# First expert blocks from attention step 20 instead of 22, with a wider spacing

## The chip, the cores and the metric

One Trainium2 chip, one of its cores. The metric is the device time of the whole kernel in microseconds, as the median of several runs. The kernel computes an attention layer with spatially reduced keys and, on its output, a mixture of eight experts, of which each row uses one.

## The reference, cut to what matters

```python
# attention: B=4, N=12288 rows, C=128; kv is pooled 4x4 to 768 keys per batch
kv_pool = kv.reshape(B, H // 4, 4, W // 4, 4, C).mean(axis=(2, 4))
k = v = kv_pool.reshape(B, -1, C) @ w_sr
s = (q @ k.transpose(0, 2, 1)) / sqrt(C)
a = softmax(s)
x = (a @ v).reshape(B * N, C)                     # 49152 rows

# experts: E=8, F=1024; each row goes to the expert of its highest logit
logits = (x / |x|) @ (emb / |emb|).T / tau
e = argmax(logits); gate = softmax(logits)[e]
out[row] = gate * (relu(x[row] @ w1[e]) @ w2[e])
```

Products are made from fp16 pairs (a high part and what is left of it), three terms for each.

## The kernel before, in words

The 49152 rows are worked through in 96 **steps** of 512 rows (`NSTEP`), 24 steps for each of the four batches. A step has four chunks of 128 rows. For each chunk TensorE makes the scores against 768 keys (`s_mm`, L608), VectorE takes the row maximum (`s_max`, L613), a small operation turns it into the bias of the exponential (`s_bias`, L625 where it is on VectorE), ScalarE takes the exponential (`s_exp`, L631), the result is cut into a high and a low fp16 part (`p_hi` L649, `p_lo` L659), both are transposed by DMAs of the SP queue (`p_t`, L664), and TensorE multiplies them with the values (`av`, L679). `x_norm` (L690, L691) and `x_mul` (L699 where it is on ScalarE, L701 where it is on VectorE) divide by the row sums. The query of a step is turned either on TensorE (`q_t`, L341) or, from step `qd` on, by a DMA (`q_turn`).

Four steps make a **group**. For each group a chain of small VectorE operations picks the expert of every row (`g_logits` and what follows; its tiles are called n3z, y and so on, with the group's number), and POOL scatters the 16 sets of 128 rows into a buffer in HBM sorted by expert (L183, `xs_rows`). From the third group on, `select` also picks four **tiles**: each a block of 512 rows of one expert that has been filled so far. A tile needs the scatters of its group plus two, is loaded by the SP queue (`load`, L1274) with its weights by POOL (`load_w`, L1258), and has eight units: first product (`l1`, L1298), ReLU high part on ScalarE (`h_hi`, L1305), low part on VectorE (`h_lo`, L1310), second product (`l2`, L1331). Then `o_out` (L1340) scales and POOL scatters the rows to the output (L183, `out_dram`). 88 tiles have 512 rows; after them smaller ones of 256 rows take what is left (18 in this run).

The keys and values of batch 1 are pooled on POOL (L365 to L386) while batch 0 is under way; step 24 needs them.

**The order** of all this is written out by a planner in the kernel's own Python (`Plan.run`): each operation has an engine, an assumed duration and a key, and whenever an engine is free it takes the ready operation of lowest key. The engines then run their lists in that order on the chip. Keys are times in the planner's scale: `TS[k]` is the key of step k, which grows by `da` for each step before `ka` and by `di` after it; `slot(k, s)` is step k plus s eighths; the other entries of `X` are offsets. Up to step `ka` the score tiles have four buffers in PSUM; there `swap_banks` (`x_swap`) gives two of them and one more bank to the experts. `x_swap` waits until the users of those banks are done. Before, tile m has the key of step `ka + m`:

```python
    for m in range(NTILE):
        k = KA + m
        TM.append(TS[k] if k <= NSTEP else TM[-1] + X["db"] * size(m - 1) / T)
```

with `ka=22`, so that 22 steps hold attention alone, 74 steps hold one tile each, and 14 tiles and the small ones follow behind the attention. A letter string in `X` deals an operation to engines: `nm` and `nm0` the bias (mixed steps and steps before `ka`), `xn` and `xn0` the product of `x_mul`, `pm` the two parts of the exponentials in the first steps (A is ScalarE, D VectorE, P POOL).

Of the kernel before, what the change touches and what calls it, by code (L numbers as in the profile page):

```python
# [36 lines left out]


X = dict(
    ka=22, da=6.919, di=15.197, db=12.403, dma=1.46, ahead=3.016, av=9.0, av0=0.39, l2=1.971, qt=5.647,  # L40
    lead=15.443, x=4.072, r=2.598, s=-2.823, p=10.466, x0=18.227, r0=19.685, s0=2.117, p0=10.054, qt0=1.742,
    pm="cabcbcacccbccbccccacaa", pl="aaaaaaaa", nm="DD", xn="A", nm0="D", xn0="DA", we="dcdadcddaddcddcd",
    h=5.625, kv=6.596, kvs=0.535, w0=-23.865, start=21.505, early=28.723, wd=10.527, xw=0.77, qd=45, qs=4.44,
    ql=8.549, v0=47.946, m=1.536, end=-1.246, ne=-9.661, ge=-97.983,
)


# [1 line left out]
def attention_moe(  # L49
# [26 lines left out]
    NSTEP = NT // Q  # L76
# [4 lines left out]
    T, TR = 512, 256  # L81
# [129 lines left out]
    class Plan:  # L211
# [8 lines left out]
        def add(self, eng, dur, key, fn, *deps, dma=None, take=None, free=None, hold=False, lands=False):  # L220
            op = Op(eng, dur, key, fn, deps, dma, take, free, hold, lands, self.stage)
            self.ops.append(op)
            return op
# [94 lines left out]
    pl = Plan()  # L318
# [4 lines left out]
    kvs = pools.enter_context(tc.tile_pool(name="kvs", bufs=1))  # L323
# [930 lines left out]
    def size(t):  # L1254
        return T if t < NA else TR

    def load_w(t):
        nc.gpsimd.indirect_dma_start(  # L1258
            out=wbuf[t % WB][:, :],
            out_offset=None,  # L1260
            in_=wprep[:, :],
            in_offset=bass.IndirectOffsetOnAxis(ap=wi_i[:, t : t + 1].bitcast(U32), axis=0),
            bounds_check=E * P - 1,
            oob_is_err=False,
        )

    def load(t):
        n = size(t)
        o = nc.sync.value_load(off_i[0:1, t : t + 1], min_val=0, max_val=NROW - n)
        x = wk2.tile([P, 2, n], F16, tag="x", name=f"x_{t}", bufs=3)  # L1270
        m = wk2.tile([P, n // P, 2], F32, tag="m", name=f"m{t}", bufs=4)
        src = xs[ds(o, n), :]
        moves = [
            nc.sync.dma_start(out=x[:, h, :], in_=src.bitcast(F16)[:, h * HP : h * HP + C], transpose=True)  # L1274
            for h in range(2)
        ]
        b = nc.sync.dma_start(out=m, in_=src[:, CG : CG + 2].rearrange("(j p) c -> p j c", p=P))
        if t < NA:
            for ins in (*moves, b):
                for key in keys[t // PER + 3 :]:  # L1280
                    tc.declare_no_dep(ins.ins, group=key, reason="rows of earlier groups only")
                tc.add_to_no_dep_group("loads", ins.ins)
        ts[t].update(x=x, m=m)

    def units(t):
        return NF * size(t) // 512

    def l1(t, u):
        n = size(t)
        fu = 512 // n  # L1290
        wt, x = wbuf[t % WB], ts[t]["x"]
        pool = ps_s if t >= NA and u % 2 else ps_h
        ph = pool.tile([P, 512], F32, tag="ph", name=f"ph{t}_{u}")
        for kk in range(fu):
            f = (u * fu + kk) * P
            terms = ((0, x[:, 0, :]), (F, x[:, 0, :]), (0, x[:, 1, :]))
            for i, (o, r) in enumerate(terms):
                nc.tensor.matmul(  # L1298
                    ph[:, kk * n : (kk + 1) * n], wt[:, o + f : o + f + P], r, start=i == 0, stop=i == 2
                )  # L1300
        ts[t]["ph", u] = ph
# [45 lines left out]
    def o_scatter(t, j):  # L1347
        scatter(out, ts[t]["m"][:, j, 1:2].bitcast(U32), ts[t]["o"][:, j, :], NT - 1, "out")


    KA = X["ka"]
    KX = KA - 1
    TS = [0.0]
# [3 lines left out]
    def slot(k, s):  # L1357

        k, s = k + int(s // 8), s % 8
        hurry = X["end"] / X["ne"] * min(max(k + s / 8 - (NSTEP - X["ne"]), 0), X["ne"])  # L1360
        return TS[k] + s / 8 * (TS[k + 1] - TS[k]) - hurry
# [4 lines left out]
    def turn(tag, bufs):  # L1366

        u = uses.setdefault(tag, [])
        return (u[-1][:1] if u else []) + (u[-bufs] if len(u) >= bufs else [])

    def took(tag, op):
        uses[tag].append([op])
        return op

    def reads(tag, *ops):
        uses[tag][-1].extend(ops)
# [6 lines left out]
    early = []  # L1383
# [248 lines left out]
    def group_ops(g, t):  # L1632
        if g == NGRP - 1:
            t -= X["ge"]
        ops = g_logits(g)
        lg = chain(t, 0.3, ops, *counted[g], *placed.get(g - 1, ()), *placed.get(g - 2, ()))
        t += 0.3 * len(ops)
        ex = add("ACT", 0.2, t, lambda: g_exp(g), lg[-1])
        rk = add("PE", 0.02, t, lambda: g_count(g), lg[-1], *chosen.get(g - 5, ()), take=f"rk{g}")
        rk = add("DVE", 0.1, t, lambda: g_counts(g), rk)  # L1640
        rk = add("PE", 0.12, t, lambda: g_rank(g), rk)
        places, gates = g_place(g)
        t += 2.0
        pc = []
        for i, fn in enumerate(places):
            deps = pc[-1:] if i else [rk, *chosen.get(g - 5, ())]
            pc.append(add("DVE", 0.2, t + 0.3 * i, fn, *deps, free=f"rk{g}" if i == 1 else None))
        gc = chain(t + 0.5, 0.3, gates, ex, pc[-1], dur=0.15)
        o = pc[0]
        t += 3.0  # L1650
        sc = [
            add("POOL", 1.28, t + 1.28 * i, lambda i=i: g_scatter(g, i), pc[-1], gc[-1], dma=0.22) for i in range(GT)
        ]
        placed[g] = [pc[-1], gc[-1], *sc]
        b = g * G // SPB
        g_last[b] = [gc[-1]]
        counted["n", g] = o
        if g >= 2:
            n = g - 2
            chosen[n] = []  # L1660
            deps = [o, *(chosen[n - 1][-1:] if n else ())]
            for i, fn in enumerate(select(n, base[(n + 3) % 3])):
                eng, dur = ("DVE", 0.15) if fn.__name__ in SELECT_DVE else ("POOL", 0.3)
                chosen[n].append(add(eng, dur, t + 0.3 * i, fn, *(chosen[n][-1:] or deps)))
        return t

    TM = []
    for m in range(NTILE):
        k = KA + m
        TM.append(TS[k] if k <= NSTEP else TM[-1] + X["db"] * size(m - 1) / T)  # L1670

    def swap_banks(last):
        nonlocal ps_s, ps_h
# [17 lines left out]
    for k in range(NSTEP):  # L1691
        if k % SPB == SPB // 2 and k // SPB + 1 < B:
            kv_ops(k // SPB + 1)
        t = step_ops(k)
        if k % G == G - 1:
            t = group_ops(k // G, t)
    x_last = add("-", 0.0, TS[NSTEP], lambda: swap_banks(True), *uses["s1"][-1], *uses["s1"][-2])
    end = counted["n", NGRP - 1]
# [5 lines left out]
    for t in range(NTILE):  # L1704
        pl.stage = sum(t >= NA + n for n in STAGES)
        s, n, nu = TM[t], t // PER, units(t)
        w = (X["di"] if KA + t < NSTEP else X["db"]) / 8
        whole = t < NA
        deps = [x_open, chosen[n][-1], *placed[n + 2]] if whole else [x_open, rest[-1], x_pads, x_dummies, *placed[NGRP - 1]]
        ld = add("SP", 3.5, s - X["lead"], lambda t=t: load(t), *deps, *turn("mx", 3), *turn("m", 4), dma=1.3 * size(t) / T)  # L1710
        took("mx", ld)
        took("m", ld)
        lw = took("wb", add("POOL", 1.35, s - X["lead"] - 1.0, lambda t=t: load_w(t), *deps[:2], *stores, *turn("wb", WB), dma=2.92))
        o1 = o2 = None
        f = 512 / size(t)
        for u in range(nu):
            key = s + (u + X["m"]) * w
            tag, swap = ("ph2", x_last) if not whole and u % 2 else ("ph", x_swap)
            o1 = took(tag, add("PE", 0.65, key, lambda t=t, u=u: l1(t, u), ld, lw, swap, o1, *turn(tag, 2)))
            k2 = key + X["l2"] * w  # L1720
            hi = took("hh", add("ACT", 0.48, k2 - X["h"], lambda t=t, u=u: h_hi(t, u), o1, *turn("hh", 4)))
            lo = took("hl", add("DVE", 0.6, k2 - X["h"] + 0.3, lambda t=t, u=u: h_lo(t, u), hi, *turn("hl", 4)))
            reads(tag, hi, lo)
            po = "xp" if not whole and t % 2 else "po"
            o2 = add("PE", 0.68, k2, lambda t=t, u=u: l2(t, u), hi, lo, o2, *(turn(po, 1) if u == 0 else ()))
            if u == 0:
                took(po, o2)
            reads("hh", o2)
            reads("hl", o2)
        reads("mx", o1)  # L1730
        o = took("o", add("DVE", 0.66 / f, k2 + 0.8, lambda t=t: o_out(t), o2, *turn("o", 2)))
        reads(po, o)
        reads("wb", o)
        sc = [
            add("POOL", 1.28, k2 + 4.0 + 1.28 * j, lambda t=t, j=j: o_scatter(t, j), o, dma=0.2) for j in range(size(t) // P)
        ]
        reads("o", *sc)
        reads("m", o, *sc)
# [39 lines left out]
```

## Time and profile before

| what | value |
|---|---|
| median of 3 runs | 2239.3 us (2238.09 to 2240.94) |
| time of the profiled execution | 2243.36 us |
| span of the profiled execution | 2241.7 us |
| TensorE busy | 1975.5 us (88%) |
| VectorE busy | 1765.4 us (79%) |
| ScalarE busy | 1531.3 us (68%) |
| POOL busy | 1464.9 us (65%) |
| mean granted TensorE clock | 0.972 |

The span is read in stages. Up to 58 us the kernel prepares keys and weights. Up to 372 us it runs attention steps alone. Around 372 to 409 us it changes over. Up to 1951 us each step goes along with one tile of the experts. Behind that only tiles are left. A line of the window view gives a stretch, its length, the busy time of TensorE (PE), its weight loads (PEld), VectorE (DVE), ScalarE (ACT) and POOL with the number of instructions in brackets, then the granted TensorE clock as a share of 2.4 GHz, the busy share of the DMA engines and GB/s. With one source line, only that line's engine is given. A line of the group view gives line, engine, operation, tiles, shapes and count, then the busy time, the mean of one in ns, and the engine's idle time before them with what ended it. A line of the chain view or the timeline gives start, duration and what ran, and in square brackets the idle time before it with what ended it. A line of the wait view gives who waited for whom, the sum in us, how often, and the longest.

### The profile page before, as it was taken

How to read it: one execution, taken by the hardware profiler on the slowest of the kernel's cores; microseconds unless marked ns; L12 is line 12 of the kernel's file. 1: busy time of each engine (PE TensorE's matmuls, PEld its weight loads, DVE VectorE, ACT ScalarE, POOL GpSimd, SP SyncE). 2: the span in 40 equal slices, each digit the busy share in tenths (PEclk: the TensorE clock that was granted, in tenths of full speed). 3: DMA queues.
4: the chain of work that ended last, by engine and by line, in shares of the span. 5: the costliest groups of instructions: out<-in, count | busy, mean ns of one | idle time of the engine just before them, and what ended most of it. 6: DMA issues, size and time to landing. Idle time of an engine off the chain costs nothing.

```text
span 2241.7 us, 57429 instructions
## 1 busy us (share of the span) xinstructions
PE 1975.5 (88%) x21516; PEld 1492.5 (67%) x21516; DVE 1765.4 (79%) x3863; ACT 1531.3 (68%) x3158; POOL 1464.9 (65%) x1932
## 2 busy tenths in 40 slices
PE   5776765988999889898999998999999999999998
PEld 4455554766777666676766776666777766776697
DVE  6877788888878878888878878888888878865655
ACT  3677776687777667776767776777777777754443
POOL 1435268877677686686686686876686576677454
PEclk9788997999999999999999999999999999999999
DMA  8897799978778678997888897978887787743233
GB/s 233 188 209 157 156 181 197 183 149 140 158 131 151 136 137 166 167 180 137 141 158 156 137 169 143 207 146 154 134 155 145 133 160 120 134 79 81 50 86 79
DMA packets 896123, 331.86 MB, mean 148 GB/s; under 512 B 842706, under 2 KB 854107, under 8 KB 894048
## 3 DMA queue, kind: packets, MB, share of 16 engines
q1 hardware_dynamic: 853504, 258.60, 64.8%
q0 software_dynamic: 39968, 68.29, 11.0%
q8 instruction: 171, 2.80, 0.5%
q10 hardware_dynamic: 2368, 1.25, 0.2%
q14 instruction: 112, 0.92, 0.1%
HBM read 170.55 MB, written 64.50 MB: 105 GB/s over the span
## 4 chain that ended last, share of the span: by engine, by line
DVE 27%; PE 27%; POOL 17%; ACT 13%; issue 12%; DMA 4%; POOLq 0%; SPq 0%; DVEq 0%; ACTq 0%
POOL xs_rows L183 8%; PE po L1331 7%; PE s L608 7%; PE ph L1298 7%; DVE plo L659 7%; DVE nm L613 6%; ACT p L631 6%; PE xp L679 5%; DVE hl L1310 5%; POOL out_dram L183 3%; ACT phi L649 2%; ACT hh L1305 2%; POOL t_part L1023 2%; ACT x L699 1%; DVE nm L625 1%
## 5 line engine op out<-in xcount | busy, mean ns | idle before, releaser
L1305 ACT ACTIVATE hh<-ph 128x512 f16<-128x512 f32 x776 | 463.2, 597 | 340.4 <-PE ph L1298 286.0
L1310 DVE SCALAR_TENSOR_TENSOR hl<-ph,hh 128x512 f16<-128x512 f32 x776 | 530.0, 685 | 141.1 <-ACT hh L1305 135.9
L1298 PE MATMUL ph<-x,wbuf 128*128 128x512 f16 (+1 forms) x2544 | 623.5, 362 | 1.8 <-DVE hl L1310 1.3
L1331 PE MATMUL po<-wbuf,hh 128*128 128x128 f16 x6208 | 610.9, 219 | 8.3 <-DVE o L1340 8.2
L1331 PE MATMUL po<-wbuf,hl 128*128 128x128 f16 x3104 | 560.2, 220 | 36.1 <-DVE hl L1310 34.4
L608 PE MATMUL s<-k,qT 128*128 128x512 f16 (+1 forms) x2304 | 454.0, 336 | 134.4 <-ACT p L631 98.4
L1331 PEld LDWEIGHTS <-hh 128*128 128x128 f16 x6208 | 498.5, 98 | 80.1 <-issue 13.2
L631 ACT ACTIVATE p<-s,nm,qa 128x768 f32<-128x768 f32 x384 | 380.2, 991 | 249.1 <-DVE nm L625 136.6
L183 POOL DMA_INDIRECT out_dram<-o,m x388 | 415.7, 1071 | 183.5 <-issue 101.0
L183 POOL DMA_INDIRECT xs_rows<-rows,pi x384 | 421.6, 1098 | 120.0 <-issue 101.6
L679 PE MATMUL xp<-v,pthi 128*128 128x137 f16 x4608 | 467.5, 227 | 24.1 <-DVE x L701 18.0
L659 DVE TENSOR_TENSOR plo<-p,phi 128x768 f16<-128x768 f32 x371 | 402.8, 1087 | 69.3 <-ACT phi L649 64.2
L679 PEld LDWEIGHTS <-pthi 128*128 128x128 f16 x4608 | 385.2, 100 | 100.5 <-issue 32.5
L608 PEld LDWEIGHTS <-qT 128*128 128x128 f16 x2304 | 228.2, 100 | 326.8 <-issue 177.8
L679 PE MATMUL xp<-v,ptlo 128*128 128x137 f16 x2304 | 444.4, 226 | 0.6 <-DMA ptlo<-plo 0.6
L613 DVE TENSOR_REDUCE nm<-s 128x1 f32<-128x768 f32 x384 | 364.9, 950 | 75.9 <-PE s L608 40.9
L1331 PEld LDWEIGHTS <-hl 128*128 128x128 f16 x3104 | 304.0, 98 | 54.8 <-DVE hl L1310 52.9
L649 ACT CAST phi<-p 128x768 f16<-128x768 f32 x380 | 315.4, 832 | 4.3
L1298 PEld LDWEIGHTS <-wbuf 128*128 128x128 f16 x2544 | 219.9, 98 | 101.6 <-issue 6.3
L679 PEld LDWEIGHTS <-ptlo 128*128 128x128 f16 x2304 | 227.1, 99 | 0.8 <-DMA ptlo<-plo 0.8
L723 POOL COPY x<-x 128x32 f32<-128x32 f32 x96 | 33.2, 345 | 198.5 <-ACT x L699 198.3
L1258 POOL DMA_INDIRECT wbuf<-w_prep,wi_i x106 | 117.0, 1104 | 56.6 <-issue 19.7
(338 smaller groups left out, 1911.7 us busy)
## 6 DMA issues: line engine op xcount, KB each, us to landing
q<-in_q_dram SPq DMA_DIRECT2D x96, 256.0 KB
kvt<-in_kv_dram SPq DMA_DIRECT2D x64, 384.0 KB
wf<-in_moe_w_dram SPq DMA_DIRECT2D x16, 512.0 KB
out_dram<-o,m POOLq DMA_INDIRECT x388
xs_rows<-rows,pi POOLq DMA_INDIRECT x384
w_prep<-wo SPq DMA_DIRECT2D x8, 514.0 KB
w_prep<-wo SPq DMA_DIRECT2D x8, 512.0 KB
x<-xs_rows SPq DMA_TRANSPOSE x212
```

What stands on the lines that cost most here:

```text
L183: ins = nc.gpsimd.indirect_dma_start(out=dst[:, :], out_offset=bass.IndirectOffsetOnAxis(ap=idx, axis=0), in_=src, in_offset=None, bounds_ ...
L608: nc.tensor.matmul(t[:, o + lo : o + hi], qs[:, l, :], r[:, lo:hi], start=i == 0, stop=i == 2)
L613: V.tensor_reduce(out=nm, in_=ks[k]["s", j], axis=AX.X, op=ALU.max, negate=True)
L631: nc.scalar.activation(out=p, in_=ks[k].pop(("s", j)), func=AF.Exp, bias=ks[k].pop(("nm", j)), scale=ks[k]["fac"],)
L649: nc.scalar.copy(out=hi, in_=p)
L659: eng.tensor_tensor(out=lo, in0=ks[k].pop(("p", j)), in1=hi, op=ALU.subtract)
L679: nc.tensor.matmul(ks[k]["xp", h][:, i, :w], l[:, c, :], r[:, c, :w], start=c == 0 and n == 0, stop=c == NCH - 1 and n == 2,)
L1258: nc.gpsimd.indirect_dma_start(out=wbuf[t % WB][:, :], out_offset=None, in_=wprep[:, :], in_offset=bass.IndirectOffsetOnAxis(ap=wi_i[:, t ...
L1298: nc.tensor.matmul(ph[:, kk * n : (kk + 1) * n], wt[:, o + f : o + f + P], r, start=i == 0, stop=i == 2)
L1305: nc.scalar.activation(out=hh, in_=ts[t]["ph", u], func=AF.Relu)
L1310: V.scalar_tensor_tensor(out=hl, in0=ts[t].pop(("ph", u)), scalar=0.0, in1=ts[t]["hh", u], op0=ALU.max, op1=ALU.subtract)
L1331: nc.tensor.matmul(po[:, j * C : (j + 1) * C], l[:, js], wt[:, o : o + P], start=first, stop=last, skip_group_check=True,)
```

## The change

The first tile is keyed to step 20 and the next ones 1.095 steps apart, until tile 22 is back at the old place (step 22 plus its number). `ka` goes from 22 to 20, and with it the change of the PSUM banks. The other entries of `X` are set anew with it. Most of them are offsets of keys: they move an operation in the lists and add none. Some deal operations otherwise: the bias goes to ScalarE for every chunk before step 20 (`nm0`) and for every second one after (`nm`); both halves of `x_mul` are on ScalarE before step 20 (`xn0`); two of the first chunks cut their exponentials on other engines (`pm`); and steps 45 to 51 turn their queries on TensorE instead of by a DMA (`qd`). What is computed stays.

```diff
 X = dict(
-    ka=22, da=6.919, di=15.197, db=12.403, dma=1.46, ahead=3.016, av=9.0, av0=0.39, l2=1.971, qt=5.647,
-    lead=15.443, x=4.072, r=2.598, s=-2.823, p=10.466, x0=18.227, r0=19.685, s0=2.117, p0=10.054, qt0=1.742,
-    pm="cabcbcacccbccbccccacaa", pl="aaaaaaaa", nm="DD", xn="A", nm0="D", xn0="DA", we="dcdadcddaddcddcd",
-    h=5.625, kv=6.596, kvs=0.535, w0=-23.865, start=21.505, early=28.723, wd=10.527, xw=0.77, qd=45, qs=4.44,
-    ql=8.549, v0=47.946, m=1.536, end=-1.246, ne=-9.661, ge=-97.983,
+    ka=20, da=7.325, di=15.283, db=8.139, dma=1.378, ahead=3.224, av=9.143, av0=0.39, l2=1.971, qt=5.395,
+    lead=17.034, x=4.15, r=5.696, s=-3.154, p=32.939, x0=15.311, r0=14.418, s0=2.027, p0=10.001, qt0=1.61,
+    pm="cabcbcacccbccbcccccdaa", pl="aaaaaaaa", nm="AD", xn="A", nm0="A", xn0="AA", kb=22.0, sp=1.095,
+    we="dcdadcddaddcddcd", h=6.436, kv=7.166, kvs=0.535, w0=-23.672, start=21.505, early=28.391, wd=14.383,
+    xw=1.141, qd=52, qs=4.44, ql=7.779, v0=45.059, m=1.592, end=-1.246, ne=-12.073, ge=-95.305,
 )
...
     for m in range(NTILE):
-        k = KA + m
-        TM.append(TS[k] if k <= NSTEP else TM[-1] + X["db"] * size(m - 1) / T)
+        k = min(KA + X["sp"] * m, X["kb"] + m)
+        TM.append(slot(int(k), k % 1 * 8) if k <= NSTEP else TM[-1] + X["db"] * size(m - 1) / T)
...
-        w = (X["di"] if KA + t < NSTEP else X["db"]) / 8
+        w = (X["di"] if X["kb"] + t < NSTEP else X["db"]) / 8
```

## Rows read from the trace of the kernel before

**Rows 1.** Windows by stage, all engines: attention alone, two mixed stretches, the tail.

```profile
246.00:372.00 126.00, 90.35 (x876) 67.80 (x875) 106.99 (x239) 94.86 (x190) 73.84 (x93) 0.92 0.92 176
...
453.00:899.00 446.00, 407.59 (x4531) 305.99 (x4531) 368.03 (x821) 331.04 (x707) 324.57 (x455) 1.00 0.76 146
899.00:1951.00 1052.00, 975.87 (x10907) 732.27 (x10905) 870.96 (x1928) 769.98 (x1619) 729.98 (x977) 1.00 0.84 151
1951.00:2142.00 191.00, 186.81 (x2089) 134.28 (x2087) 115.42 (x239) 88.84 (x172) 126.62 (x168) 1.00 0.34 73
```

**Rows 2.** The same windows, exponentials of L631 alone (four for each step).

```profile
246.00:372.00 126.00, 36.15 (x37) 0.92 0.92 176
...
453.00:899.00 446.00, 82.88 (x84) 1.00 0.76 146
899.00:1951.00 1052.00, 198.66 (x201) 1.00 0.84 151
```

**Rows 3.** The same window, ReLUs of L1305 alone (eight for each tile).

```profile
453.00:899.00 446.00, 98.56 (x165) 1.00 0.76 146
```

**Rows 4.** Chain that ended last, in order of time: TensorE's pieces at full clock.

```profile
433.89 0.97 PE s L608 x6
434.87 0.67 PE po L1331 x12
435.54 0.65 PE ph L1298 x3
436.18 1.09 PE xp L679 x18
...
445.93 0.44 PE pq L341 x4
```

**Rows 5.** Waits of PE from 58 to 372 us.

```profile
PE s L608 <- ACT p L631: 43.0, 31, 4.0
```

**Rows 6.** Waits of PE from 899 to 1951 us.

```profile
PE s L608 <- ACT p L631: 41.2, 51, 2.9
PE po L1331 <- DVE hl L1310: 19.3, 26, 3.2
```

**Rows 7.** Timeline around the change of the banks, PE and then DVE.

```profile
384.14 0.39 PE L679 MATMUL xp<-v,pthi 128*128 128x137 f16 x2 [12.26 <-DVE x L701]
...
375.37 1.31 DVE L739 TENSOR_SCALAR n3z<-ss 128x16 int32<-128x16 int32 x1
...
383.56 0.43 DVE L701 TENSOR_TENSOR x<-xp,rn 128x272 f32<-128x272 f32 x1
```

**Rows 8.** Attention alone, 246 to 346 us: the window, then groups of DVE and ACT.

```profile
246.00:346.00 100.00, 73.94 (x748) 57.44 (x748) 86.55 (x200) 78.30 (x166) 50.73 (x63) 0.93 0.90 172
...
L625 DVE TENSOR_SCALAR nm<-nm,qa 128x1 f32<-128x1 f32 x28 | 5.6, 201 | 0.0
...
L701 DVE TENSOR_TENSOR x<-xp,rn 128x272 f32<-128x272 f32 x7 | 3.1, 441 | 0.1
...
L728 ACT ACTIVATE junk<-x 128x128 f32<-128x128 f32 x26 | 7.9, 307 | 0.0
...
L728 ACT ACTIVATION_READ_ACCUMULATOR junk<-x 128x1 f32 x26 | 5.1, 195 | 0.0
...
L699 ACT ACTIVATE x<-xp,rn 128x136 f32<-128x136 f32 x14 | 4.4, 369 | 0.9 <-DVE nm L625 0.6 <-DVE rn L691 0.3
```

**Rows 9.** POOL from 300 to 453 us, and the load that waits for its last scatter.

```profile
300.00:453.00 153.00, 113.07 (x1177) 86.18 (x1175) 128.02 (x277) 103.72 (x224) 117.64 (x157) 0.91 0.94 186
...
L1258 POOL DMA_INDIRECT wbuf<-w_prep,wi_i x4 | 4.8, 1203 | 0.9 <-issue 0.8
L183 POOL DMA_INDIRECT out_dram<-o,m x4 | 4.2, 1051 | 1.2 <-issue 1.2
...
373.79 1.54 POOL L183 DMA_INDIRECT xs_rows<-rows,pi  x1 [0.17 <-issue]
...
379.82 2.48 SPq L1274 DMA_TRANSPOSE x<-xs_rows  x2
```

## The prediction

> **What bounds the kernel now.** I read the windows by stage first, because a mean over the kernel hides that it has three regimes. In the mixed stretches TensorE is busy 407.59 of 446.00 us and 975.87 of 1052.00 us, over 91% at full clock (1.00), and in the tail 186.81 of 191.00; with attention alone it is busy 90.35 of 126.00, and at a granted clock of 0.92 [rows 1]. So what counts at the end is TensorE's work, plus the time in which it stands still. Next come the counts, which give the pace. From 246 to 372 us there are 37 exponentials, four to a step: 126.00 / 9.25 = 13.62 us for a step of attention alone. From 453 to 899 us there are 84, or 21 steps: 21.24 us for a mixed step; from 899 to 1951 us 201, or 50.25 steps: 20.94 us [rows 1, 2]. The first mixed stretch holds 165 / 8 = 20.6 tiles, about one a step [rows 3].
>
> The chain gives TensorE's work at full clock. A step is 4 x (0.97 + 1.09) + 0.44 = 8.68 us, a tile 8 x (0.65 + 0.67) = 10.56 us [rows 4]. A mixed step thus holds 19.24 us of work and some 2.0 us of anything else; a step of attention alone holds 8.68 us of work in 13.62, so 4.94 us are left open. Who leaves them open: TensorE waits for the exponential (43.0 us up to 372) [rows 5], which itself follows VectorE and ScalarE in turn, busy 86.55 and 78.30 of 100 us [rows 8]. In the mixed steps the same wait and the one for the low part of ReLU are the largest left (41.2 and 19.3 us in 1052) [rows 6].
>
> **The change, part by part.** *The earlier, wider start.* Tile m gets the key of step min(20 + 1.095 m, 22 + m); both are equal at m = 2 / 0.095 = 21. So steps 20 and 21, now attention alone, become mixed, and the same 22 tiles lie on 24 steps. No work is added. Before: 2 x 13.62 + 22 x 21.24 = 494.5 us. After, three ways. If the 2.0 us of other time belong to each mixed step: 24 x 10.68 + 22 x 10.56 = 488.6, a gain of 5.9. If they belong to the tiles: 24 x 8.68 + 22 x 12.56 = 484.6, a gain of 9.9. If the open time of a step falls in a straight line with the tiles in it, from 4.94 at none to 2.0 at one, the sum doesn't depend on where they lie: a gain of 0. I take 5.9, the middle one, because the stalls that TensorE has left in mixed steps hang on the scores, that is on the step [rows 6].
>
> *The bank swap* moves along from step 22 to 20. It now costs a stall of 12.26 us, ended by x_mul on VectorE, which ran at 383.56, behind the chain of group 3 that began at 375.37 [rows 7]. Before, the chain's key is slot(16, 6.39) + 19.685 + 3 = 138.9 planner us and that of the x_norm in front of this x_mul 148.6; after, slot(16, 6.39) + 14.418 + 3 = 140.5 and 142.6 for step 18. The chain still sorts ahead, so I expect the stall again. x_mul goes to ScalarE there, which saves its own 0.43 us and its turn in VectorE's list. Between 0 and 8 us could go (8 if the chain falls behind it: 383.56 - 375.37); I take a gain of 1.
>
> *Queries of steps 45 to 51 on TensorE.* Seven times 0.44 us of TensorE [rows 4], 3.1 us in a stage where TensorE is the bound. The pace of the stretch that turns on TensorE is only 21.24 - 20.94 = 0.30 us a step longer than of the one that turns by DMA [rows 1, 2], which gives 2.1. Cover could make it 0. I take a loss of 2. The SP queue loses seven transposes by this; nothing on TensorE waits for them now.
>
> *Bias on ScalarE, mixed steps* (every second chunk). VectorE loses 2 x 0.20 us a step, ScalarE gains about as much: its trace shows no such operation; the nearest rows are the one-column accumulator read (195 ns) and the 128-column activation (307 ns) [rows 8]. I take 0.2, being nearest in size, and keep 0.31. VectorE is at 870.96 / 1052 = 83%, ScalarE at 73% [rows 1]; so the move eases the fuller one by 0.4 of some 17.3 us a step. If VectorE alone set the pace that were 75 x 0.4 = 30 us, but TensorE does; of its stalls (41.2 + 19.3 in the longer stretch) a few per cent may go. I take a gain of 3, between -3 and 8.
>
> *The cut of the exponentials* (p from 10.466 to 32.939) now ranks about behind the experts' operations of two steps on, as late as the product av that needs it. ReLU parts go first, which helps the second wait of [rows 6], while exponentials wait longer for a free buffer, which lengthens the first. Signs oppose; 0, with 8 us to either side (an eighth of 41.2 + 19.3).
>
> *Steps 0 to 19: bias and x_mul on ScalarE.* For 100 us, VectorE loses 28 x 0.201 + 7 x 0.441 = 8.7 us and falls to 77.9; ScalarE gains 28 x 0.195 + 14 x 0.369 = 10.6 and rises to 88.9 [rows 8]. The two change places. VectorE's 86.55 was no full engine and the step was set by turns between the two; a hand-over less for each chunk helps, a fuller ScalarE harms. I take 0, from -8 (a gain of 0.4 us a step) to +7.5 (below). The two chunks of pm and the wider spacing of the weight preparation (wd) move the same work within the stage; taken at 0 as well.
>
> *The tail.* Keys of the tail's tiles come closer (db). Only 191.00 - 186.81 = 4.2 us are open there [rows 1]; 0, at most 4 either way. xw enters a latency that no operation uses; it does nothing.
>
> **Sum.** -5.9 - 1 + 2 - 3 = -7.9 us. Against the profiled execution (2243.36 us, of which the span is 2241.7) that is 2235.5; the median of the runs was 2239.3, 4.1 lower, so it becomes **2231**.
>
> **Rivals.**
> *A. ScalarE becomes the bound of attention alone (slower).* If the fuller engine can't be kept busier than VectorE's 86.55% now, the stage grows with ScalarE's share: at 0.195 us for the bias by 88.9 / 86.55 = 1.027, times 20 x 13.62 = 272 us: 7.5. At 0.307 us ScalarE comes to 78.3 + 8.6 + 5.2 = 92.1, ratio 1.064, 17.4 us. It decides from where ScalarE passes 86.55 of 100, which both prices do. With the rest of the sum: 2239 to 2249, at the middle 2244, and at the upper price clearly slower. For it: the two prices. Against it: ScalarE's idle time now ends mostly on VectorE, which this same edit unloads. The Trainium skill speaks for this rival (ScalarE: Activation LUTs, rules for kernel authors): simple products and sums belong on VectorE, and an ACTIVATE costs about 0.3 us before its elements. The 369 ns for 136 columns agree roughly; by that figure, an estimate, the rival would come out at its upper end.
> *B. POOL is late for step 24 (no gain to slower).* From 300 to 453 us POOL is busy 117.64 of 153. Before step 24 fall tiles 0 to 3 instead of 0 and 1: two more times 1.20 + 4 x 1.05 = 5.4 us, 10.8 in all [rows 9], so 128 of some 147, while it also pools the keys that step 24 needs. If all of it lands ahead of them: -7.9 + 10.8 = +3, 2242.
> *C. The first tiles can't start earlier (the change doesn't do what it says).* The load of tile 0 went out at 379.82, just behind group 2's last scatter at 373.79 [rows 9]. If those scatters come no sooner, steps 20 and 21 run without a tile and the 5.9 are lost: 2237. Against it: r0 falls from 19.685 to 14.418, and the group's chain with it by about 0.9 steps.
> *D. More than I count:* the swap's chain falls behind x_mul (7 more) and the exchange of engines pays (8): 2216 to 2224.
>
> **How the numbers follow.** Forecast (2225 to 2236) 0.42; A 0.25; B 0.08; C 0.13; D 0.12. The range takes in most of A and half of D: 2218 to 2248. About 0.2%, 4.5 us, is what a measurement here can tell. Faster than 2234.8: most of the forecast (0.39), all of D, a little of A and C (0.04): 0.55. Slower than 2243.8: half of A and some of B and of what I left out: 0.20. The rest, 0.25, is within.
>
> **What would show it.** Right: fewer than 22 steps ahead of the first ReLU of a tile, that ReLU some 15 to 25 us before its old place; step 44 reached 4 to 10 us sooner; the stretches from there on as before, but for seven steps at +0.3. Steps of attention alone within 0.4 us of 13.62. The swap stall still 8 to 12 us. Wrong: ScalarE at 89% with steps over 14 us (A); a TensorE stall at step 24 ended by the keys of batch 1 (B); the first ReLU of a tile at its old time (C). If the mixed pace itself moves by more than 0.2 us a step, my terms for the bias and the cut of the exponentials were mis-sized, since 75 steps multiply them.

## The result and the profile after

The changed kernel takes 2272.35 us (median of 2264.22 to 2278.28), the kernel before 2240.12 beside it: a ratio of 1.0138, 95% interval 1.0098 to 1.0177. It is slower by 1.4%, about 32 us; 2231 was forecast, in a range that ended at 2248. The profiled execution took 2264.22 us (span 2262.5), the shortest of its runs, so its trace accounts for 21 of the 32 us. What the longer runs add can't be read from it.

The windows by stage of the changed kernel answer to [rows 1]; the columns are the same:

```profile
246.00:372.00 126.00, 86.44 (x782) 65.25 (x781) 88.17 (x170) 98.40 (x224) 73.97 (x92) 0.82 0.78 162
...
453.00:899.00 446.00, 413.06 (x4564) 311.85 (x4562) 369.76 (x800) 351.11 (x761) 314.27 (x435) 0.98 0.77 146
899.00:1951.00 1052.00, 976.80 (x10892) 734.66 (x10890) 857.88 (x1810) 796.03 (x1726) 730.09 (x989) 0.99 0.80 151
1951.00:2142.00 191.00, 185.10 (x2073) 133.21 (x2071) 120.61 (x264) 93.79 (x189) 126.93 (x172) 1.00 0.39 81
```

The exponentials alone, in the same windows, answer to [rows 2]:

```profile
246.00:372.00 126.00, 30.74 (x31) 0.82 0.78 162
453.00:899.00 446.00, 86.07 (x87) 0.98 0.77 146
899.00:1951.00 1052.00, 197.89 (x200) 0.99 0.80 151
```

Attention alone has become slower: 31 exponentials in 126 us instead of 37, or 16.26 us a step instead of 13.62. The mixed pace has not: 446 / 21.75 = 20.51 and 1052 / 50 = 21.04 us a step, against 21.24 and 20.94. The granted clock of the first stretch fell from 0.92 to 0.82.

The starts of the first exponentials of steps 0, 19, 44 and 95 in the timelines cut the span into four parts. Three kernels below (e1, e8 and e16) run ScalarE's and VectorE's operations in the same order up to step 18, and differ by up to 5 us in the first part; e5 keeps every list of the kernel before, and its 44 to 95 take 1066 us, 6 fewer. Less than that is not read from one profile.

| us | steps 0 to 19 | 19 to 44 | 44 to 95 | after that |
|---|---|---|---|---|
| before | 286 | 534 | 1073 | 291 |
| changed | 309 | 527 | 1073 | 294 |
| e2, both engine moves alone | 311 | 532 | 1077 | 291 |
| e1, changed without them | 282 | 534 | 1111 | 290 |
| e13, both moves in the old lists | 287 | 535 | 1071 | 293 |
| e6, changed lists, moves undone | 310 | 532 | 1071 | 294 |
| e14, bias alone, planned | 293 | 524 | 1064 | 293 |
| e3, early start alone | 284 | 546 | 1066 | 293 |
| e15, start and earlier groups | 294 | 532 | 1097 | 290 |
| e4, changed, weights as before | 295 | 528 | 1095 | 292 |
| e8, changed, all engines as before | 286 | 539 | 1084 | 292 |
| e16, as e8 and p as before | 281 | 533 | 1075 | 291 |

So the loss sits in steps 0 to 19 (+23), before the first tile. From there to step 44, where the start and the swap lie, 7 us came back. The windows of that first part, before and after:

```profile
58.40:344.20 285.80, 202.18 (x1812) 149.04 (x1810) 230.75 (x511) 213.94 (x422) 126.98 (x129) 0.86 0.84 177
59.30:368.40 309.10, 212.25 (x1831) 154.71 (x1829) 221.35 (x425) 243.94 (x534) 150.83 (x157) 0.81 0.79 170
```

TensorE was busy 10 us longer for nearly the same matmuls, at a granted clock of 0.81 instead of 0.86. So up to some 10 of the 23 us may have come through the clock. Whether the clock fell because TensorE waited more, or for another reason, no run separates.

### The profile page after: what moved, and what is told of

The parts are those of the page before. It is cut to its first block, busy times and chain, and to the rows that moved or that the text cites. A ratio compares the mean times of both kernels' runs of the same rounds, so it can differ in the third digit from the quotient of the medians.

```text
span 2262.5 us, 57421 instructions
## 1 busy us (share of the span) xinstructions
PE 1990.0 (88%) x21544; PEld 1503.8 (66%) x21544; DVE 1734.6 (77%) x3609; ACT 1605.7 (71%) x3440; POOL 1461.1 (65%) x1933
## 4 chain that ended last, share of the span: by engine, by line
PE 33%; DVE 21%; ACT 16%; POOL 15%; issue 12%; DMA 2%; POOLq 0%; ACTq 0%; DVEq 0%; SPq 0%
PE po L1331 9%; PE s L608 9%; PE ph L1298 9%; ACT p L631 6%; POOL xs_rows L183 6%; PE xp L679 6%; DVE nm L613 4%; DVE plo L659 4%; DVE hl L1310 4%; POOL out_dram L183 3%; ACT hh L1305 3%; ACT phi L649 2%; POOL t_part L1023 1%; ACT x L699 1%; ACT junk L728 1%
## 5 line engine op out<-in xcount | busy, mean ns | idle before, releaser
L1305 ACT ACTIVATE hh<-ph 128x512 f16<-128x512 f32 x776 | 461.8, 595 | 331.9 <-PE ph L1298 276.1
L608 PE MATMUL s<-k,qT 128*128 128x512 f16 (+1 forms) x2304 | 466.2, 343 | 145.7 <-ACT p L631 114.4
L631 ACT ACTIVATE p<-s,nm,qa 128x768 f32<-128x768 f32 x384 | 380.1, 990 | 167.5 <-DVE nm L625 74.6
L659 DVE TENSOR_TENSOR plo<-p,phi 128x768 f16<-128x768 f32 x370 | 395.5, 1074 | 29.0 <-ACT phi L649 28.2
L1331 PEld LDWEIGHTS <-hl 128*128 128x128 f16 x3104 | 305.5, 98 | 43.2 <-DVE hl L1310 41.2
L699 ACT ACTIVATE x<-xp,rn 128x136 f32<-128x136 f32 x384 | 122.0, 371 | 39.0 <-DVE rn L691 25.2
```

What stands on the lines that cost most here:

```text
L608: nc.tensor.matmul(t[:, o + lo : o + hi], qs[:, l, :], r[:, lo:hi], start=i == 0, stop=i == 2)
L631: nc.scalar.activation(out=p, in_=ks[k].pop(("s", j)), func=AF.Exp, bias=ks[k].pop(("nm", j)), scale=ks[k]["fac"],)
L659: eng.tensor_tensor(out=lo, in0=ks[k].pop(("p", j)), in1=hi, op=ALU.subtract)
L699: nc.scalar.mul(x[:, i, :], xp[:, i, : C + E], rn[:, i, :])
L1305: nc.scalar.activation(out=hh, in_=ts[t]["ph", u], func=AF.Relu)
L1331: nc.tensor.matmul(po[:, j * C : (j + 1) * C], l[:, js], wt[:, o : o + P], start=first, stop=last, skip_group_check=True,)
```

## What the slow stretch looks like

The window that answers to [rows 8], and groups of ScalarE in it (in the changed kernel the bias has its own line, L623):

```profile
246.00:346.00 100.00, 69.50 (x609) 52.49 (x608) 72.57 (x141) 76.21 (x176) 55.36 (x67) 0.80 0.79 163
...
L631 ACT ACTIVATE p<-s,nm,qa 128x768 f32<-128x768 f32 x23 | 22.8, 993 | 11.1 <-PE s L608 5.7 <-DVE plo L659 5.4
...
L623 ACT ACTIVATE nm<-nm,scales,qa 128x1 f32<-128x1 f32 x24 | 9.3, 388 | 2.0 <-DVE nm L613 1.5 <-DVE y L757 0.5
...
L699 ACT ACTIVATE x<-xp,rn 128x136 f32<-128x136 f32 x22 | 7.0, 372 | 7.3 <-DVE rn L691 3.8 <-PE pq L341 3.5
```

Two things to see. A bias costs 388 ns on ScalarE, above both of the rows that I had bounded it by (195 and 307). And no engine is full: ScalarE is busy 76.21 of 100 us, less than the 78.30 of before, VectorE 72.57, TensorE 69.50. They wait for one another. TensorE's wait for exponentials from 58 to 372 us, the one of [rows 5], was 43.0 us in a window with 85 of them; with 78 it is now:

```profile
PE s L608 <- ACT p L631: 48.5, 28, 5.4
```

ScalarE's timeline shows what stands in front of an exponential:

```profile
293.82 0.99 ACT L631 ACTIVATE p<-s,nm,qa 128x768 f32<-128x768 f32 x1 [1.59 <-PE s L608]
294.71 0.30 ACT L728 ACTIVATE junk<-x 128x128 f32<-128x128 f32 x1
294.91 0.19 ACT L728 ACTIVATION_READ_ACCUMULATOR junk<-x 128x1 f32 x1
295.01 0.30 ACT L728 ACTIVATE junk<-x 128x128 f32<-128x128 f32 x1
295.21 0.19 ACT L728 ACTIVATION_READ_ACCUMULATOR junk<-x 128x1 f32 x1
295.30 0.71 ACT L561 ACTIVATE q<-q,qa 128x512 f32<-128x512 f32 x1
295.91 0.37 ACT L623 ACTIVATE nm<-nm,scales,qa 128x1 f32<-128x1 f32 x1
296.19 0.82 ACT L649 CAST phi<-p 128x768 f16<-128x768 f32 x1
296.91 0.39 ACT L623 ACTIVATE nm<-nm,scales,qa 128x1 f32<-128x1 f32 x1
297.20 0.82 ACT L649 CAST phi<-p 128x768 f16<-128x768 f32 x1
299.03 0.39 ACT L623 ACTIVATE nm<-nm,scales,qa 128x1 f32<-128x1 f32 x1 [1.01 <-DVE nm L613]
299.32 0.82 ACT L649 CAST phi<-p 128x768 f16<-128x768 f32 x1
300.04 0.99 ACT L631 ACTIVATE p<-s,nm,qa 128x768 f32<-128x768 f32 x1
```

Between two exponentials, 294.71 to 300.04, stand sums of squares, a query, three biases and three casts; the third bias waits a whole microsecond for its maximum, and a cast and the next exponential stand behind it. A score buffer is not free until its exponential has run. Worked out from the timelines for the chunks of steps 4 to 18, the mean time from the end of a row maximum to the start of its exponential is 8.7 us before, 10.7 in the changed kernel, 11.2 in e2, 10.7 in e6, 9.2 in e13, and 7.0 in e1.

The bias isn't what an exponential waits for. Counted in order (the n-th maximum, bias, exponential, cast and low part belong to one chunk), the exponential at 300.04 had its bias since 289.98. It writes into one of four buffers (`p`), and the low part on VectorE that empties this buffer, four chunks back, ended at 299.80. In steps 6 to 18 that low part ended later than the exponential's own bias for all 52 chunks, before and after; the exponential began 0.5 us behind it before, and 0.7 after. Already before, in the window of [rows 8], ScalarE's idle time in front of exponentials ended for the most part on a low part:

```profile
L631 ACT ACTIVATE p<-s,nm,qa 128x768 f32<-128x768 f32 x29 | 28.7, 991 | 18.8 <-DVE plo L659 10.8 <-PE s L608 3.4 <-DVE rn L690 3.1
```

The low part needs the cast, and the cast is what the slow lists put late: from the end of an exponential to the cast of its result pass 8.0 us before and 8.5 in e13, but 12.0 in the changed kernel, 11.4 in e6 and 11.2 in e2. Without biases and x_mul, 11.7 operations of ScalarE lie between the two before and in e13, 16.1 in the changed kernel and in e6, 15.2 in e2. A buffer is then held for 16.6 us instead of 14.5, and four chunks, a step, take 17.4 instead of 15.0. This is read from the order and the times; no run moved the casts alone, and e4 holds its buffers for only 14.7 us although 16.0 operations stand there.

## The experiments

**Is it the engines, the weights, or the start?** Theory A: the bias and the first half of x_mul, moved to ScalarE, lengthen the steps. Rival W: the weight preparation, spread farther by wd, does.

```diff
 e1 (on the changed kernel)
-nm0="A", xn0="AA"
+nm0="D", xn0="DA"
 e2 (on the kernel before)
-nm0="D", xn0="DA"
+nm0="A", xn0="AA"
 e3 (on the kernel before)
-ka=22,
+ka=20, kb=22.0, sp=1.095,
+        k = min(KA + X["sp"] * m, X["kb"] + m)      # and the rest of the diff outside X
 e4 (on the changed kernel)
-wd=14.383, w0=-23.672
+wd=10.527, w0=-23.865
```

> The changed kernel, but bias (nm0) and x_mul (xn0) of the steps before 20 dealt as before: bias on VectorE, every second x_mul on VectorE; the lists are planned anew with that. Theory A (the bias of 384 ns and the second x_mul on ScalarE lengthen the attention steps from 14.9 to 16.3 us): steps 0 to 19 come back to 285 us and the kernel to about 2248, or under 2240 where the earlier start pays its 7 us as well. Theory W (the weight preparation, spread farther, lengthens the steps): no change, 2268 to 2275.

> The kernel before, but bias and x_mul of the steps before 22 on ScalarE as in the change; nothing else but the planning anew. Theory A: 20 to 26 us slower, about 2263. Theory W: 2240, within 5 us.

> The kernel before with the early, wider start alone (ka 20, the new rule for the tiles' keys); engines and all other offsets as before. By the terms of the prediction (5.9 for the start, 1 for the swap): 7 us faster, about 2233. If the start itself is at fault (POOL late for step 24, or tiles that can't start): 2240 to 2255.

> The changed kernel with the spacing of the weight preparation as before (wd 10.527, w0 -23.865). Theory W: steps 10 to 13 lose their 17 to 21 us and the kernel comes to 2255 or less. Theory A: no change, 2268 to 2275.

Measured beside 2242.74 of the kernel before: e1 2277.32 (ratio 1.0153, 1.0135 to 1.0172), e2 2266.28 (1.0110, 1.0093 to 1.0127), e3 2248.85 (1.0042, 1.0023 to 1.0061), e4 2267.78 (1.0112, 1.0095 to 1.0129). The parts of the span say more than the totals. Putting the two moves in costs steps 0 to 19 25 us (286 to 311), taking them out of the changed kernel gives 27 back (309 to 282): the same size in two surroundings, as theory A has it. But e1 as a whole gained nothing, because its mixed steps from 44 on took 1111 us instead of 1073. W predicted no loss in e2 and is not the main cause; undoing the spacing did shorten steps 0 to 19 by 14, and was taken back by the mixed steps (1095). So the price of the two moves depends on what else the list holds: 25 us in e2, 9 in e4, with the same spacing. The start alone is 6 us slower, not 7 faster.

**Is it ScalarE's time or the list?** A changed letter in X alters both: where an operation runs, and the order that the planner writes for all five engines. The next kernels keep every list as it is and change only the engine that issues the operation (in e5, e6 and e13 the planner still counts with the old engine); e7 adds an operation instead.

```diff
 e5 (before, lists kept)
-        if in_turn("nm", k, NQ * k + j) == "ACT":
+        if k < KA:
 e13 (before, lists kept): as e5, and
-        if in_turn("xn", k, 2 * k + h) == "ACT":
+        if k < KA or in_turn("xn", k, 2 * k + h) == "ACT":
 e6 (changed, lists kept)
-        if in_turn("nm", k, NQ * k + j) == "ACT":
+        if k >= KA and in_turn("nm", k, NQ * k + j) == "ACT":
-        if in_turn("xn", k, 2 * k + h) == "ACT":
+        if (k >= KA or h) and in_turn("xn", k, 2 * k + h) == "ACT":
 e7 (before, lists kept), behind each exponential
+        if k < KA:
+            nc.scalar.activation(out=idle_t, in_=idle_t, func=AF.Identity, scale=..., bias=...)
```

> The kernel before with every engine's list as it was, but the bias of steps 0 to 21 issued on ScalarE at the place that the list gives it (384 ns there in the changed kernel, 203 on VectorE before). Theory A: ScalarE's 0.38 us in front of each exponential lies on the turn of score, maximum, exponential: 88 times 0.18 us longer and a fuller ScalarE, 10 to 20 us slower. Theory P (it is the planning anew that harms, not the engine): 2240, within 5 us.

> The changed kernel with its lists as they are, but bias and the first half of x_mul of steps 0 to 19 issued on VectorE at the same places. Theory A: steps 0 to 19 shorten by 15 to 24 us and the kernel comes to 2245 to 2257. Theory P: 2268 to 2275, no change.

> The kernel before with its lists as they are and one more operation: behind each exponential of steps 0 to 21 ScalarE computes one column of a tile that nobody reads, about as long as the bias there (0.38 us, 34 us of ScalarE in all). If it is ScalarE's load that costs: 15 to 25 us slower. If it is the longer way from the maximum to the exponential: within 6 us of 2240.

> The kernel before with its lists as they are, but bias and x_mul of steps 0 to 21 both issued on ScalarE at the places that the lists give them. It holds the same operations on the same engines as the run with both dealt over and planned anew (24 us slower). If the lists are what costs: 3 to 10 us slower than the kernel before, step 19 reached by 352 us. If ScalarE's fuller time is: 16 to 28 us slower, step 19 at 360 or later.

e5 2247.98 beside 2242.75 (1.0019, 1.0002 to 1.0036), e7 2246.93 (1.0022, 1.0005 to 1.0040), e13 2247.96 beside 2243.84 (1.0027, 1.0013 to 1.0041), e6 2268.02 beside 2242.75 (1.0108, 1.0065 to 1.0151). This turns theory A over: 4 to 5 us where it asked for 10 to 28. e13 and e2 run the same operations on the same engines in steps 0 to 19; e13 needs 287 us for them and e2 311. And the changed kernel's lists stay slow (310) when the operations go back to VectorE. In e13 the stretch from 246 to 346 us reads:

```profile
246.00:346.00 100.00, 73.01 (x729) 56.44 (x727) 77.77 (x164) 88.86 (x210) 46.51 (x60) 0.91 0.88 169
...
L631 ACT ACTIVATE p<-s,nm,qa 128x768 f32<-128x768 f32 x29 | 28.9, 1001 | 8.4 <-PE s L608 4.5 <-PE xp L679 2.9 <-DVE plo L659 1.0
...
L623 ACT ACTIVATE nm<-nm,scales,qa 128x1 f32<-128x1 f32 x29 | 11.6, 400 | 1.7 <-DVE nm L613 1.4
```

ScalarE is at 88.86 of 100 us and still makes 29 exponentials, where the changed kernel makes 23 at 76.21. In e6 the same window has ScalarE at 68.25:

```profile
246.00:346.00 100.00, 68.72 (x586) 52.35 (x587) 74.27 (x175) 68.25 (x143) 53.43 (x65) 0.80 0.81 161
```

A fuller ScalarE costs the kernel 4 to 5 us (e5, e7, e13), 1 us of it at most in steps 0 to 19; the order in the lists costs the 23 there.

**Which of the two writes the slow list?**

```diff
 e14 (before)
-nm0="D"
+nm0="A"
 e17 (before)
-xn0="DA"
+xn0="AA"
 e18 (changed)
-xn0="AA"
+xn0="DA"
```

> The kernel before with the bias alone of steps 0 to 21 dealt to ScalarE and the lists planned with it. If the lists for a bias on ScalarE are what costs: 15 to 25 us slower than the kernel before, step 19 at 359 to 369 us. If it takes x_mul as well: within 8 us of it.

> The kernel before with the first half of x_mul of steps 0 to 21 dealt to ScalarE and planned with it, bias as before. If the list for x_mul is the rest of the 25 us: steps 0 to 19 take 300 to 308 us instead of 286, and the kernel is 12 to 22 us slower. If only the two moves together fill ScalarE in the planner's account: steps 0 to 19 within 7 us of 286.

> The changed kernel with the first half of x_mul of steps 0 to 19 on VectorE again, planned anew, all else as changed. If the list for x_mul is the rest, or the two only do it together: steps 0 to 19 take 286 to 296 us instead of 309. If the bias alone does it here: 303 to 312. The total also moves with the mixed steps, whose lists are planned anew: 2240 to 2275.

e14 takes 2234.15 beside 2243.84: 0.9970, 0.9953 to 0.9987, the one kernel on this chip that beats both. Its steps 0 to 19 take 293 us, 7 more than before, and its later ones 524 and 1064, 19 fewer, though no entry that belongs to them was touched: the planner carries the early order on, and ScalarE's operations of steps 24 to 43 stand in another order than before. So the bias alone doesn't write the whole of the slow list. The two that would settle the rest ran on another chip, on which the kernel before took 2568.82: there e17 is 2571.77 (0.9987, 0.9955 to 1.0020) and e18 2541.19 (0.9892, 0.9848 to 0.9936). Steps 0 to 19 took 300 us in e17 and 297 in e18, but the same part of e13, e14 and e15 was 3 to 15 us longer on such a chip than here, so neither verdict holds: whether x_mul alone writes the slow list or only both together stays open. Two things speak for both together. Less those 3 to 15 us, an estimate, e17 and e18 would take 285 to 297 and 282 to 294 here. And between an exponential and its cast, without biases and x_mul, stand 13.8 operations with the bias moved (e14) and 13.4 with x_mul moved (e17), against 11.7 before and 15.2 with both (e2). The changed kernel itself wasn't timed on that chip.

**What holds the start back?** In e3 the first ReLU of a tile came at 410 us, after group 2's last scatter at 375. e15 brings the groups' chains and the tiles' loads forward with it.

```diff
 e15 (on e3)
-x0=18.227, r0=19.685, lead=15.443
+x0=15.311, r0=14.418, lead=17.034
```

> The kernel before with the early start and x0 15.311, r0 14.418, lead 17.034, engines as before. The start alone left tile 0 at 410 us, behind group 2's last scatter at 375. If that wait keeps the start from paying: scatters of group 2 end 10 us sooner or more, the first ReLU of a tile is 15 us sooner than 410, and the kernel is 2 to 9 us faster than the kernel before. If not: 5 to 20 us slower.

2275.27 beside 2243.84 (1.0145, 1.0125 to 1.0164). Group 2's last scatter went out at 371 instead of 375, not 10 us sooner; the first ReLU came at 392; steps 19 to 44 took 532 us instead of 546, and steps 44 to 95 took 1097 instead of 1066. The earlier tile paid 14 us where it was to pay, and the mixed steps took more than that. In the changed kernel POOL's last scatter of group 2, and then the load that waits for it, answer to [rows 9]:

```profile
371.58 1.00 POOL L183 DMA_INDIRECT xs_rows<-rows,pi  x1 [0.17 <-issue]
```

```profile
376.76 2.59 SPq L1274 DMA_TRANSPOSE x<-xs_rows  x2
```

373.79 and 379.82 before: the first tile is keyed two steps sooner and starts at its old time, its ReLU at 391.5 us instead of 392.5.

**The mixed steps.** e8 deals bias and x_mul as before in all steps; e16 also puts p back.

```diff
 e8 (on e1)
-nm="AD"
+nm="DD"
 e16 (on e8)
-p=32.939
+p=10.466
```

> The changed kernel with bias and x_mul dealt as before in all steps, the mixed ones too (nm DD, nm0 D, xn0 DA), planned anew. The run with only the first steps so dealt was 6 us ahead of the kernel before at step 64 and lost 41 us from there to step 95. If the bias on ScalarE in mixed steps was the cause of that: about 2235. If the place of the planned cuts of the exponentials (p) is: 2265 to 2280.

> The changed kernel with bias and x_mul dealt as before in all steps and p back at 10.466. With p at 32.939 this took 2258 and lost 12 us to the kernel before between steps 44 and 95. If the later cut is the cause: those steps come back to 1073 us and the kernel to 2238 to 2246. If not: 2250 to 2265.

e8 2257.85 beside 2242.75 (1.0061, 1.0038 to 1.0083), e16 2240.92 beside 2243.84 (0.9994, 0.9976 to 1.0012). With e1 at 2277 that is 19 us for the bias of mixed steps and 17 for p. Yet the changed kernel has both edits, and its steps 44 to 95 take the 1073 us of before. In these lists they cost, in those they don't: none of the two has a price of its own.

e11, e9, e12 and e10 are the kernels of e13, e14, e15 and e17 on a chip where the kernel before took 2569.5. Their ratios there are 0.9994, 1.0009, 1.0031 (0.9993 to 1.0069) and 0.9992. The third is the kernel that costs 1.0145 here, with an interval of 1.0125 to 1.0164: the price of an order on one chip isn't its price on another.

## Why the prediction was wrong

- **Steps 0 to 19, bias and x_mul on ScalarE**: the failed step. I took 0, at most +7.5, and measured +23. Twice mis-sized: a bias lasts 384 to 400 ns, not 195, of which the next operation overlaps 0.1, so that in e5 it adds 0.27 us of busy time (213.94 to 234.57 for 76 of them); and I priced an operation by its duration on its engine, although the edit goes through the planner. The price of the operations was near (e13: 1 us in these steps, 4 in all), that of the order in the list was missing (e6: 24 us with the operations undone). The planner's code counts 0.2 us for a bias on ScalarE; whether a list planned with the measured time would be better was not tried. The wider wd, taken at 0 as well, was worth 14 us in this stage (e4); pm was not tried alone.
- **Rival A** had the side and the stage, but not the cause. Its sum for ScalarE, 88.9 of 100 us, meets what e13 shows (88.86) by luck, with a bias at half its duration; and at that the pace holds. In the changed kernel ScalarE is at 76.21. With 400 ns its formula would even have given the loss in the right size: (78.3 + 28 x 0.4 + 5.2) / 86.55 = 1.094 of 272 us, 26 us. A sum that fits is no proof of its mechanism. The Trainium skill's figure (ScalarE: Activation LUTs, rules for kernel authors), about 0.3 us for an ACTIVATE before its elements, was nearer than my 195 ns and still below the 388. The Trainium skill gives it there for a bias read from memory; here the scale is read from memory as well.
- **The earlier start**: 5.9 expected. Steps 19 to 44 gained 7 with the swap, but 5 against e2, which has no earlier start and the same engines, and e3 lost 12 there. The kernels with the start need 527 to 546 us, those without 524 to 535. So the middle one of my three ways isn't borne out; nothing here tells its gain from 0, the third of them, in which the open time falls in a straight line with the tiles.
- **Rival C** came true for the first tile (391.5 us), for another reason than it gave: the last scatter of group 2 did come two steps earlier (in step 19, not 21), and the steps became slower.
- **Rival B**: TensorE has no stall at step 24 for the keys of batch 1 in the changed kernel. POOL is busy 104.30 of 153 us from 300 to 453 us, less than the 117.64 of before.
- **The swap**: the stall of 12.26 us behind x_mul [rows 7], which I expected to stay, is gone; in its place TensorE waits for the load of tile 0 and for the expert choice of a group:

```profile
384.42 1.46 PE L1298 MATMUL ph<-x,wbuf 128*128 128x512 f16 x6 [2.75 <-DMA x<-xs_rows]
...
391.91 0.18 PE L825 MATMUL rk<-ones,oh 128*128 128x1 f16 x1 [6.03 <-DVE oh L811]
```

- **Queries of steps 45 to 51**: 2 us of loss expected, none seen: steps 44 to 52 take 180 us in both traces. **Mixed bias and p**: 3 us of gain and 0 expected; 1073 us in both. TensorE's waits of [rows 6] fell a little, to 35.9 us for exponentials and 18.3 for the low part, from 41.2 and 19.3; the term for p had the first one grow. A new one of 8.0 us, of the first product for a low part, is larger than what they lost. **Tail**: +3, within its bound of 4.
- **The range**: it was built from durations and their bounds, and no term stood for a new order of the lists. e1, e4, e8 and e15 show that such an order moves the mixed steps alone by 12 to 38 us.

## What to carry to other kernels

Where a planner writes the order, a changed number or letter is not a local edit: it rewrites every engine's list, and the time comes from the lists. To price an operation, issue it on the other engine in the unchanged list (1 us here, in steps 0 to 19); to price an order, keep its list and undo the operations (24 us). A stage in which no engine is full is read from the places in a list: see what stands between a result and the operation that frees its buffer, here between an exponential and the cast of its result.

## What was not expected of the hardware

A one-column ScalarE operation with a scale and a bias from memory took 384 to 400 ns, longer than a 128-column square (302 to 325 ns in the same windows, and the read of its sum is an operation of its own, 194 to 214). The next operation begins 0.28 to 0.29 us after it, as the timeline above shows. And the kernel is sensitive to the chip: on two others the kernel before took about 2569 us instead of 2243. In the trace of e17, taken there, engines often stand idle with nothing that the profile names, as TensorE from 1000 to 1900 us:

```profile
PE s L608 <- ACT p L631: 25.4, 38, 3.2
PE po L1331 <- issue: 18.4, 32, 1.6
```

On the first chip that second wait isn't among the longest of the kernel before. Why those chips differ was not tried.
